# Dilated and sliding-window attention with a gated convolution layer: sequence positions reordered by residue mod 12, dilated q and k transposed without a cast, weights cast by the load, and a new order of steps

## Chip, core and metric

The kernel runs on one core of a Trainium2 chip. The metric is device time in microseconds (us) of one launch, the median of several runs. The core's engines work side by side, each through its own list of instructions: PE (TensorE: matmuls and transposes), DVE (VectorE), ACT (ScalarE), POOL (GpSimd) and SP, whose queue here only issues DMAs.

## What is computed

There are 8 batches, 8 heads, 576 positions and head size 64. Heads 0 to 3 ("plain") see the last 32 positions; heads 4 to 7 ("dilated") see every fourth of the last 128. The output of attention is x, which goes through a gate and two projections:

```python
scores = scale * np.matmul(q, k.transpose(0, 1, 3, 2))
mask_plain = (rel >= 0) & (rel < window)                                  # window 32
mask_dil = (rel >= 0) & (rel < window * dilation) & (rel % dilation == 0)  # dilation 4
attn = softmax(np.where(masks, scores, -1e9))
x = np.matmul(attn, v)              # heads side by side: (8, 576, 512)
for k in range(5):                  # causal, per channel
    gate_pre += conv_w[k] * xp[:, k:k + S, :]
out = (sigmoid(gate_pre) * (x @ w_val)) @ w_out
```

## The kernel before

The work is cut into 32 pairs of heads, four to a batch: two plain, then two dilated. Iteration i of the loop at L485 works on pair i. Each engine runs its instructions in the order in which this loop writes them, so that order is set by hand.

**Loading.** A group is the four plain or the four dilated heads of a batch. `load_group` (L99) loads a group from SP's queue, two groups ahead. q and k come as 128 partitions of four neighbouring rows (512 of 576 positions), and the last 64 positions in four small DMAs each, into `q_rest` and `k_rest`. The first two groups are loaded in halves of two heads. `prep_group` (L141) has POOL cast q and k of the next pair to bf16 and bring v into place: for plain heads a copy of 32 overlapping rows inside `vP`, for dilated heads casts into `vA` and `vB`.

**One pair.** `trans_in` (L256) transposes q and k on PE: four transposes of 128 rows (L261) and one of 64 (L266) for each; DVE copies q (L273) and ACT copies k (L278 or L280) out of PSUM. The position order after it is by residue mod 4, so a dilated head's keys are neighbours. `scores` (L291) multiplies for one half of the pair's work and ACT takes the exponential (L318); `apply_mask` (L322) multiplies with a 0/1 mask on DVE; `attn_v` (L333) multiplies with v, which carries a column of ones for the row sums; `normalize` (L350) divides on DVE (L359, L360). `trans_x` (L367) transposes x on PE (L380) and DVE copies it to `xT` (L382).

**The dense part.** For each 128-channel chunk c and half G of the positions, `conv` (L387) does the five-tap convolution as matmuls with diagonal matrices (L405) and ACT takes tanh (L413); `val` (L416) is x @ w_val (L420), multiplied with the gate on DVE (L426); `out_tile` (L432) projects 128 rows (L435), ACT copies them to `osb` (L440) and SP stores them (L446). `conv`, `val` and `out_tile` share two PSUM buffers, `ps_moe`. Once a batch's four pairs are there, its 8 `val` and 4 or 5 `out_tile` items go into a list, and `pop_dense` takes from it by a budget at three places in an iteration. In an iteration the order is: first scores, transposes of the pair before's x, its first conv, second scores, dense work, transposes of the next q, first half of attention, second conv, transposes of the next k, dense work, second half, dense work.

**At the start** POOL builds the masks, then (`setup_conv_w`, L221) the twenty diagonal matrices `conv_diag` (L232); in iteration 2 it casts the two weight matrices (L243, L245), loaded as fp32.

Of the kernel before, what the change touches and what calls it, by code (L numbers as in the profile page):

```python
# [22 lines left out]
def kernel(  # L23
# [9 lines left out]
):  # L33
    nc = tc.nc
# [5 lines left out]
    DIL = 4  # L40
    T = S // DIL
    scale = 1.0 / float(D) ** 0.5
    NCH = Dm // 128
    TM = 128
    TR = T - TM
    CP = T + 2
    NB = 6
# [3 lines left out]
    KOFF = 32  # L51
    NP = B * NCH
# [21 lines left out]
    mask_p = consts.tile([128, 4, 24], BF16, name="mask_p")  # L74
    mask_d = consts.tile([128, HB], BF16, name="mask_d")
    NKT = 3
    kTs = [consts.tile([128, KOFF + S + 16], BF16, name=f"kT{i}") for i in range(NKT)]
# [3 lines left out]
    vPs = [consts.tile([128, NB, 4, VS], FP32, name=f"vP{i}") for i in range(NVP)]  # L81
# [3 lines left out]
    vBst = [consts.tile([128, 4, 2, 64], FP32, name=f"vBst{i}") for i in range(NVD)]  # L85
    NXT = 3
    xTs = [xt_pool.tile([128, NCH, DIL, CP], BF16, name=f"xT{i}") for i in range(NXT)]
# [6 lines left out]
    w_st = [consts.tile([128, NCH, Dm], FP32, name=f"w_st{i}") for i in range(2)]  # L94
# [4 lines left out]
    def load_group(g):  # L99
        b, dil = g // 2, g % 2  # L100
        h0 = dil * 4
        t = {}
        parts = [(0, 2), (2, 4)] if g < 2 else [(0, 4)]
        for name in ("q", "k"):
            t[name] = qk_pool.tile([128, 4, 4 * D], FP32, name=f"{name}_nat")
            t[name + "r"] = qk_pool.tile([64, 4, D], FP32, name=f"{name}_rest")
        if dil:
            t["vst"] = vst_pool.tile([128, 4, 4 * D], FP32, name="v_st")
        for (a, e) in parts:
            for name, src in (("q", q), ("k", k)):  # L110
                nc.sync.dma_start(
                    out=t[name][:, a:e, :],
                    in_=src[b, h0 + a:h0 + e, 0:4 * TM, :].rearrange("h (p r) d -> p h (r d)", r=4),
                )
                for r in range(4):
                    nc.sync.dma_start(  # L116
                        out=t[name + "r"][16 * r:16 * r + 16, a:e, :],
                        in_=src[b, h0 + a:h0 + e, 4 * TM:S, :].rearrange(
                            "h (p r) d -> r p h d", r=4)[r],
                    )  # L120
            if not dil:
                vt = vPs[b % NVP]
                for h in range(a, e):
                    nc.sync.dma_start(
                        out=vt[32:128, :, h, 0:D],
                        in_=v[b, h0 + h].rearrange("(t p) d -> p t d", p=96),
                    )
            else:
                nc.sync.dma_start(
                    out=t["vst"][:, a:e, :],  # L130
                    in_=v[b, h0 + a:h0 + e, 0:4 * TM, :].rearrange("h (p r) d -> p h (r d)", r=4),
                )
                for hf in range(2):
                    nc.sync.dma_start(
                        out=vBst[b % NVD][64 * hf:64 * hf + 48, a:e, :, :].rearrange("p h j d -> p h (j d)"),
                        in_=v[b, h0 + a:h0 + e, 4 * 96:S, :].rearrange(
                            "h (p f j) d -> f p h (j d)", f=2, j=2)[hf],
                    )
        grp_tiles[g] = t

    def prep_group(g, a):  # L141

        b, dil = g // 2, g % 2
        t = grp_tiles[g]
        e = a + 2
        for name in ("k", "q"):
            if a == 0:
                t[name + "b"] = qb_pool.tile([128, 4, 4, D], BF16, name=f"{name}_b")
                t[name + "rb"] = qb_pool.tile([64, 4, D], BF16, name=f"{name}_rb")
            nc.gpsimd.tensor_copy(  # L150
                t[name + "b"][:, :, a:e, :],
                t[name][:, a:e, :].rearrange("p h (r d) -> p r h d", r=4))
            nc.gpsimd.tensor_copy(t[name + "rb"][:, a:e, :], t[name + "r"][:, a:e, :])
        if True:
            if not dil:
                vt = vPs[b % NVP]
                for h in range(a, e):
                    nc.gpsimd.tensor_copy(
                        vt[0:32, 1:NB, h, 0:D], vt[96:128, 0:NB - 1, h, 0:D])
            else:  # L160
                nc.gpsimd.tensor_copy(
                    vAs[b % NVD][:, a:e, :, 0:D],
                    t["vst"][:, a:e, :].rearrange("p h (r d) -> p h r d", r=4))
                nc.gpsimd.tensor_copy(
                    vBs[b % NVD][:, a:e, :, 0:D], vBst[b % NVD][:, a:e, :, :])

    load_group(0)
# [8 lines left out]
    for kt in kTs:  # L176
        nc.vector.memset(kt[:, 0:KOFF], 0.0)
        nc.vector.memset(kt[:, KOFF + S:], 0.0)
    for et in ets:
        nc.vector.memset(et[:, 2 * HB:], 1.0)  # L180
    nc.vector.memset(vPs[0][:, :, :, D:D + 1], 1.0 - 2.0 ** -9)
    nc.vector.memset(vPs[0][0:32, 0, :, 0:D + 1], 0.0)
# [14 lines left out]
    band(mask_p, [[1, 4], [4, 24]], 32)  # L197

    prep_group(0, 0)

    for i in range(NVD):
        nc.vector.memset(vAs[i][:, :, :, D:D + 1], 1.0)
# [353 lines left out]
```

## Time and profile before

| what | us |
|---|---|
| median of 3 runs | 262.7 |
| lowest and highest run | 261.54 and 263.8 |
| the profiled execution | 261.05 |
| its span, first to last instruction | 259.0 |
| PE busy | 204.8 (79%) |
| DVE busy | 132.8 (51%) |
| POOL busy | 109.3 (42%) |
| ACT busy | 106.5 (41%) |

The profile shows one execution. Its span is 2.05 us shorter than its time. Its 40 slices are 6.5 us each, and a digit is an engine's busy share in tenths. In rows of the time order stand start, length, engine, line, operation, and in brackets the idle time before it with what ended it; "x6" means that six such instructions are put together. In rows of waits stand the engine and line that waited, what it waited for, and total, number and longest. PEld is PE's loading of weights (the stationary operand), which runs beside matmuls. "ps_tr", "ps_sc" and "ps_moe" are PSUM buffers for transposes, for scores and attention, and for the dense part.

### The profile page before, as it was taken

The numbers are of one execution on the slowest core, as the hardware profiler recorded it, in microseconds if no ns is written. First come the engines' busy times: TensorE is split into PE (matmuls) and PEld (weight loads), VectorE is DVE, ScalarE is ACT, GpSimd is POOL, SyncE is SP. The second block draws the span as 40 slices with busy tenths as digits, with TensorE's granted clock in tenths as the row PEclk, the third lists the DMA queues.
The fourth block names the chain that finished last, engine by engine and source line by source line (L and its number), as shares of the span: only waits on it lengthen the run. The fifth ranks groups of instructions, "written<-read, shape, count | busy, mean of one in ns | idle before, by whom it ended". The sixth has DMA issues, their size and how long they took to land.

```text
span 259.0 us, 5708 instructions
## 1 busy us (share of the span) xinstructions
PE 204.8 (79%) x2117; PEld 131.8 (51%) x2132; DVE 132.8 (51%) x345; ACT 106.5 (41%) x198; POOL 109.3 (42%) x238
## 2 busy tenths in 40 slices
PE   0461586389997999899988998899889998999793
PEld 0240353255655665565556655656555655565551
DVE  5150243135657665575656565657445646665440
ACT  1221133042464345535553545264525455445312
POOL 2699908998044343625263426082626061000000
PEclk9999999999999999999999999999979999999999
DMA  3555889850758566595667564858582761112033
GB/s 93 147 163 158 231 272 288 254 136 0 213 174 225 124 188 197 147 240 172 197 185 186 166 207 128 223 152 247 170 217 48 224 191 40 48 37 67 16 81 121
DMA packets 60725, 41.28 MB, mean 159 GB/s; under 512 B 31509, under 2 KB 55061, under 8 KB 60698
## 3 DMA queue, kind: packets, MB, share of 16 engines
q1 hardware_dynamic: 60688, 40.91, 55.7%
q8 instruction: 16, 0.26, 0.4%
q14 instruction: 11, 0.09, 0.1%
q10 hardware_dynamic: 10, 0.01, 0.0%
HBM read 31.47 MB, written 9.44 MB: 158 GB/s over the span
## 4 chain that ended last, share of the span: by engine, by line
PE 68%; DVE 9%; SPq 8%; DMA 5%; ACT 3%; issue 3%; POOL 2%; POOLq 0%; ACTq 0%
PE ps_moe L405 16%; PE ps_moe L420 14%; PE ps_moe L435 12%; PE ps_tr L380 6%; DVE xT L382 5%; PE ps_sc L314 5%; PE ps_tr L261 5%; PE ps_sc L345 5%; SPq L116 5%; DMA q_rest<-in_q_dram 3%; PE ps_tr L266 3%; POOL w_out_b L245 2%; DMA q_nat<-in_q_dram 2%; PE ps_sc L310 2%; ACT kT L280 1%
## 5 line engine op out<-in xcount | busy, mean ns | idle before, releaser
L405 PE MATMUL ps_moe<-xT,conv_diag 128*128 128x288 bf16 (+1 forms) x384 | 54.2, 280 | 18.5 <-DVE xT L382 17.1
L413 ACT ACTIVATE gate<-ps_moe 128x288 bf16<-128x288 f32 x64 | 26.2, 410 | 101.7 <-PE ps_moe L405 101.7
L150 POOL CAST k_b<-k_nat 128x512 bf16<-128x512 f32 x32 | 20.7, 648 | 83.1 <-DMA k_nat<-in_k_dram 40.7
L318 ACT ACTIVATE et<-ps_sc 128x576 bf16<-128x576 f32 x64 | 41.6, 651 | 16.3 <-PE ps_sc L310 11.8
L405 PEld LDWEIGHTS <-conv_diag 128*128 128x128 bf16 x384 | 32.5, 101 | 26.7 <-issue 10.0
L426 DVE SCALAR_TENSOR_TENSOR y_all<-gate,ps_moe 128x288 bf16<-128x288 bf16 x64 | 28.4, 452 | 31.0 <-PE ps_moe L420 29.9
L420 PE MATMUL ps_moe<-xT,w_val_b 128*128 128x288 bf16 x256 | 41.7, 305 | 0.5 <-ACT osb L440 0.2
L360 DVE TENSOR_TENSOR xn<-ps_sc,rec 96x384 bf16<-96x384 f32 (+1 forms) x64 | 35.6, 555 | 2.2
L435 PE MATMUL ps_moe<-w_out_b,y_all 128*128 128x512 bf16 x129 | 35.0, 380 | 0.8
L261 PE MATMUL ps_tr<-ident,q_b 128*128 128x128 bf16 x128 | 13.8, 237 | 23.4 <-POOL q_b L150 23.4
L420 PEld LDWEIGHTS <-w_val_b 128*128 128x128 bf16 x256 | 24.1, 103 | 10.5 <-issue 2.2
L440 ACT COPY osb<-ps_moe 128x512 f32<-128x512 f32 x36 | 21.1, 585 | 18.6 <-PE ps_moe L435 16.9
L331 DVE TENSOR_TENSOR et<-et,mask_d 128x576 bf16<-128x576 bf16 x32 | 17.2, 537 | 20.1 <-ACT et L318 20.1
L382 DVE COPY xT<-ps_tr 128x576 bf16<-128x576 bf16 x32 | 14.6, 458 | 22.3 <-PE ps_tr L380 22.0
L314 PE MATMUL ps_sc<-qT,kT 64*128 64x96 bf16 (+1 forms) x320 | 20.0, 223 | 4.7 <-ACT kT L280 3.1
L273 DVE COPY qT<-ps_tr 128x576 bf16<-128x576 bf16 x32 | 14.4, 451 | 17.5 <-PE ps_tr L266 17.5
L261 PEld LDWEIGHTS <-q_b 128*128 128x128 bf16 x128 | 9.5, 105 | 26.1 <-POOL q_b L150 23.9
L331 DVE TENSOR_TENSOR et<-et,mask_p 128x576 bf16<-128x576 bf16 x32 | 16.3, 511 | 10.6 <-ACT et L318 10.1
L345 PEld LDWEIGHTS <-et 128*128 128x128 bf16 x384 | 17.7, 101 | 5.5 <-DVE et L331 0.6
L314 PEld LDWEIGHTS <-kT 64*128 64x128 bf16 x320 | 9.1, 97 | 22.1 <-issue 10.0
L380 PE MATMUL ps_tr<-ident,xn 96*128 96x96 bf16 (+2 forms) x192 | 19.8, 217 | 0.6 <-DVE xn L360 0.6
L150 POOL CAST q_b<-q_nat 128x512 bf16<-128x512 f32 x32 | 19.4, 606 | 0.0
(55 smaller groups left out, 220.8 us busy)
## 6 DMA issues: line engine op xcount, KB each, us to landing
q_nat<-in_q_dram SPq DMA_DIRECT2D x14, 512.0 KB, 4.5
k_nat<-in_k_dram SPq DMA_DIRECT2D x14, 512.0 KB, 4.8
vP<-in_v_dram SPq DMA_DIRECT2D x32, 144.0 KB, 3.4
v_st<-in_v_dram SPq DMA_DIRECT2D x7, 512.0 KB, 4.5
out_dram<-osb SPq DMA_DIRECT2D x8, 256.0 KB, 2.5
out_dram<-osb SPq DMA_DIRECT2D x8, 224.0 KB, 2.7
out_dram<-osb SPq DMA_DIRECT2D x8, 192.0 KB, 2.3
vBst<-in_v_dram SPq DMA_DIRECT2D x14, 96.0 KB, 4.1
```

What stands on the lines that cost most here:

```text
L150: nc.gpsimd.tensor_copy(t[name + "b"][:, :, a:e, :], t[name][:, a:e, :].rearrange("p h (r d) -> p r h d", r=4))
L261: nc.tensor.transpose(out=ps[:, r * T:r * T + TM], in_=t[name + "b"][:, r, a:a + 2, :], identity=ident,)
L314: nc.tensor.matmul(out=ps[:, hh, col:col + w], lhsT=lhsT, rhs=rhs, start=True, stop=True)
L318: nc.scalar.activation(out=e3, in_=ps[:, :, 0:HB], func=AF.Exp, scale=scale)
L331: nc.vector.tensor_tensor(out=e3, in0=e3, in1=m, op=ALU.mult)
L345: nc.tensor.matmul(out=ps[:, hh, j * AVS:j * AVS + D + 1], lhsT=et[:, hh * HB + col:hh * HB + col + 128], rhs=rhs, start=True, stop=True)
L360: nc.vector.tensor_tensor(out=xn[0:R, 3 * hf:3 * hf + 3, :, :].rearrange("p n h d -> p h n d"), in0=av[:, :, :, 0:D], in1=rec[0:R, :, :, N ...
L380: nc.tensor.transpose(out=o, in_=xn[0:w, 3 * hf + j, :, :], identity=ident[0:w, 0:w])
L405: nc.tensor.matmul(out=ps[:, o * T:(o + n) * T], lhsT=conv_diag[:, c, K - 1 - m, :], rhs=xt[:, c, r:r + n, off:off + T], start=(idx == 0), ...
L420: nc.tensor.matmul(out=ps[:, 0:HB], lhsT=w_val_b[:, mc, c * 128:(c + 1) * 128], rhs=xt[:, mc, 2 * G:2 * G + 2, 2:], start=(mc == 0), stop= ...
L426: nc.vector.scalar_tensor_tensor(out=y_all[:, c, b * S + G * HB:b * S + (G + 1) * HB], in0=gates.pop((b, c, G)), scalar=1.0, in1=ps[:, 0:H ...
L435: nc.tensor.matmul(out=ps, lhsT=y_all[:, c, 128 * n:128 * n + 128], rhs=w_out_b[:, c, :], start=(c == 0), stop=(c == NCH - 1),)
```

## The change

Positions are now ordered by residue mod 12, as 12 runs of 48. q and k lie in 96 partitions. For plain heads each partition holds 6 neighbouring rows of each head; POOL casts them and six transposes of 96 rows take the place of five. For dilated heads two heads lie side by side in 96 partitions of 12 rows each; there is no cast: PE transposes the upper bf16 half of every fp32 number (`hi_bf16`), two rows at a time, and the two halves of the array then hold two residues of one head, not two heads. The blocks of dilated scores are 120 and 48 wide, not 128 and 32. The small rest loads and casts are gone. For the first pair q is loaded from ACT's queue and q and k are cast on DVE. `conv_diag` is made on DVE, one product for each chunk. The weights are loaded from POOL's queue by DMAs that cast to bf16, and the factor 0.5 of w_out moves to the copy of the output. conv has 9 and 5 matmuls for its halves, where it had 6 and 6, over as many columns. An output tile is stored in runs of up to 48 rows, not 144.

The order in an iteration is now: first scores, dense work, transposes of x, second scores, a conv of the half that was queued before, k's transposes, first half of attention, the next conv, q's transposes, dense work, second half, dense work. A conv carries a time from which it may be taken.

```diff
+                (eng or nc.gpsimd).tensor_copy(
+                    t[(name, a)],
+                    t[name][:, a:e, :].rearrange("p h (j d) -> p j h d", j=6))
...
-    load_group(0)
+    load_group(0, ((0, 2),), q_eng=nc.scalar)
...
+    prep_pair(0, nc.vector)
+    load_group(0, ((2, 4),))
+    load_group(1)
...
-        for c in range(NCH):
-            for kk in range(K):
-                nc.gpsimd.tensor_scalar(
-                    out=conv_diag[:, c, kk, :], in0=ident,
-                    scalar1=conv_w_sb[:, c, kk:kk + 1], scalar2=None, op0=ALU.mult,
-                )
+    def make_conv_diag(c):
+        nc.vector.tensor_tensor(
+            out=conv_diag[:, c, :, :],
+            in0=ident[:, None, :].to_broadcast([128, K, 128]),
+            in1=conv_w_sb[:, c, :, None].to_broadcast([128, K, 128]),
+            op=ALU.mult)
...
-            nc.sync.dma_start(out=st, in_=src.rearrange("(c p) n -> p c n", p=128))
...
+            nc.gpsimd.dma_start(out=dst, in_=src.rearrange("(c p) n -> p c n", p=128))
...
+        if not dil:
+            for j in range(6):
+                nc.tensor.transpose(
+                    out=ps[:, j * 96:(j + 1) * 96], in_=t[(name, a)][:, j, :, :],
+                    identity=ident[0:96, 0:96])
+        else:
+            src = t[name].rearrange("p h x -> p (h x)")
+            pv = ps.rearrange("p (h c e u) -> p h c e u", h=2, c=2, e=3)
+            for w2 in range(6):
+                o = a * 384 + w2 * 128
+                nc.tensor.transpose(
+                    out=pv[:, :, w2 % 2, w2 // 2, :], in_=hi_bf16(src[:, o:o + 128]),
+                    identity=ident[0:96, 0:96])
...
+            r0 = 6 * G - m
+            n_wrap = max(0, -r0)
+            if n_wrap:
+                pieces.append((m, 0, W12 - n_wrap, 1, n_wrap))
+            pieces.append((m, n_wrap, max(r0, 0), 2, 6 - n_wrap))
...
-            f = 128 * n + p
-            b, r, t = f // S, (f % S) // T, f % T
-            w = min(128 - p, T - t)
+            b, w, u = f // S, (f % S) // U, f % U
+            r = min(128 - p, U - u)
...
+        dense.extend(v0 + v1[:2] + o0[:1] + v1[2:] + o0[1:] + o1)
...
+    def pop_conv(i):
+        if convs and convs[0][0] < i:
+            run(convs.pop(0)[1])
...
-        budget[0] = min(budget[0] + amount, 2.0)
-        while dense and budget[0] >= COST[dense[0][0]] * 0.5:
+        budget[0] = min(budget[0] + amount, 1.5)
+        while dense and budget[0] >= COST[dense[0][0]] * 0.6:
...
+    def push_conv(i, t):
+        b, c = pair_info(i)[0:2]
+        for G in range(2):
+            convs.append((t + 0.5 * G, ("c", b, c, G)))
...
         scores(i, 0)
-        if i > 0:
-            trans_x(i - 1)
-            pb, pc = pair_info(i - 1)[0:2]
-            convs += [("c", pb, pc, 0), ("c", pb, pc, 1)]
-            if pc == NCH - 1:
-                queue_batch(pb)
-        apply_mask(i, 0)
         if i == 0:
             setup_conv_w()
-        if i == 2:
-            cast_weights()
-        pop_conv()
+        pop_dense(0.5)
+        if i > 0:
+            trans_x(i - 1)
+            push_conv(i - 1, i)
+            if c == 0:
+                queue_batch(b - 1)
+        apply_mask(i, 0)
+        if i < NCH:
+            make_conv_diag(i)
         scores(i, 1)
-        pop_dense(0.5)
+        pop_conv(i)
         apply_mask(i, 1)
         if i + 1 < NP:
-            trans_in(i + 1, "q")
+            trans_in(i + 1, "k")
         attn_v(i, 0)
         normalize(i, 0)
-        pop_conv()
+        pop_conv(i + 0.5)
         if i + 1 < NP:
-            trans_in(i + 1, "k")
+            trans_in(i + 1, "q")
         pop_dense(0.5)
         attn_v(i, 1)
         normalize(i, 1)
-        pop_dense(0.97)
+        pop_dense(1.0)
```

Three places show how instructions move. A number behind a name tells buffers apart. First POOL at the start, from the end of pair 1's preparation on (the `vP` copy) to that of pair 2 (`k_nat_194` and `v_st_196` are its loads). Before:

```order
L158 COPY vP0_107<-vP0_107 32x5x64 x2
L232 TENSOR_SCALAR conv_diag_121<-ident_96,conv_w_sb_120 128x128 x20
L150 CAST k_b_358<-k_nat_194 128x4x128
L153 CAST k_rb_359<-k_rest_195 64x128
L150 CAST q_b_362<-q_nat_192 128x4x128
L153 CAST q_rb_363<-q_rest_193 64x128
L161 CAST vA0_109<-v_st_196 128x8x64
```

Now, from pair 1's casts of k and q to pair 2's v:

```order
L147 CAST k_b_199<-k_nat_123 96x768
L147 CAST q_b_201<-q_nat_122 96x768
L151 COPY vP0_107<-vP0_107 32x2x5x64
L184 MEMSET mask_d_99 128x120
L185 AFFINE_SELECT mask_d_99<-mask_d_99 128x120
L189 AFFINE_SELECT mask_d_99<-mask_d_99 128x120
L214 COPY mask_d_99<-mask_d_99 128x120
L184 MEMSET mask_d_99 128x48
L237 DMA w_val_b_120<-in_moe_w_val_dram 128x4x512
L237 DMA w_out_b_121<-in_moe_w_out_dram 128x4x512
L154 CAST vA0_109<-v_st_162 128x8x64
```

The twenty `conv_diag` products and pair 2's casts of q and k have left POOL; the mask for dilated heads and the two weight loads now stand between pair 1's and pair 2's preparation.

Second SP's queue, the loads of group 1 (dilated heads of batch 0). Before, the first of its two halves:

```order
L111 DMA q_nat_192<-in_q_dram 128x2x256
L116 DMA q_rest_193<-in_q_dram 16x2x64 x4
L111 DMA k_nat_194<-in_k_dram 128x2x256
L116 DMA k_rest_195<-in_k_dram 16x2x64 x4
L129 DMA v_st_196<-in_v_dram 128x2x256
L134 DMA vBst0_113<-in_v_dram 48x2x128 x2
```

Now all of it, with the first load of group 2 behind:

```order
L126 DMA k_nat_161<-in_k_dram 96x2x768
L126 DMA q_nat_160<-in_q_dram 96x2x768
L130 DMA v_st_162<-in_v_dram 128x4x256
L134 DMA vB_st_163<-in_v_dram 64x4x128 x2
L113 DMA k_nat_194<-in_k_dram 96x4x384
```

Twenty-six issues have become five, and k goes first.

Third PE in iteration 5 (the second plain pair of batch 1), at the transposes of x (`xn`); of each kind of instruction the first is shown, the repeats are left out. Before:

```order
L435 MATMUL ps_moe_786<-w_out_b_123,y_all_118 128x512
L314 LDWEIGHTS kT2_102
L314 MATMUL ps_sc_805<-qT_741,kT2_102 128x96
L380 LDWEIGHTS xn_749
L380 MATMUL ps_tr_813<-ident_96,xn_749 128x4x24
L405 LDWEIGHTS conv_diag_121
L405 MATMUL ps_moe_822<-xT1_116,conv_diag_121 128x288
L314 LDWEIGHTS kT2_102
L314 MATMUL ps_sc_831<-qT_741,kT2_102 128x96
```

Now:

```order
L287 MATMUL ps_sc_666<-qT_623,kT2_102 128x96
L412 LDWEIGHTS w_val_b_120
L412 MATMUL ps_moe_674<-xT0_113,w_val_b_120 128x288
L379 LDWEIGHTS xn_600
L379 MATMUL ps_tr_680<-ident_96,xn_600 128x12x8
L287 LDWEIGHTS kT2_102
L287 MATMUL ps_sc_689<-qT_623,kT2_102 128x96
L397 LDWEIGHTS conv_diag_119
L397 MATMUL ps_moe_697<-xT0_113,conv_diag_119 128x288
L256 LDWEIGHTS k_nat_352
```

Before, the conv behind the transposes reads what they wrote (`xT1`, batch 1). Now a val group stands ahead of the transposes and the second scores behind them, and the conv that follows reads `xT0`: it is the last conv of batch 0. The last row is the next, dilated, pair's k, loaded as weights straight from the fp32 load.

More of the change, by code (lines that the diff above doesn't have):

```diff
@@ L121, in load_group @@
[L121 to L128, printed above, removed]
+                    out=t["k"][:, a:e, :],
+                    in_=k[b, a:e].rearrange("h (p j) d -> p h (j d)", j=6))
+                for f in range(2):
+                    q_eng.dma_start(
+                        out=t["q"][48 * f:48 * f + 48, a:e, :],
+                        in_=q[b, a:e].rearrange("h (u f j) d -> f u h (j d)", f=2, j=6)[f])
@@ L139, in load_group, with prep_pair @@
[L139 to L143 removed]
+                        out=t["vBst"][64 * f:64 * f + 64, a:e, :, :].rearrange("p h j d -> p h (j d)"),
+                        in_=v[b, 4 + a:4 + e, 4 * TB:S, :].rearrange(
+                            "h (p f j) d -> f p h (j d)", f=2, j=2)[f])
+    def prep_pair(i, eng=None):
+        b, c, dil, g, a = pair_info(i)
         t = grp_tiles[g]
         e = a + 2
[L146 to L165, printed above, removed]
@@ L439, in out_tile @@
         osb = out_pool.tile([128, Dm], FP32, name="osb")
-        nc.scalar.copy(out=osb, in_=ps)
+        nc.scalar.mul(out=osb, in_=ps, mul=0.5)
         p = 0
```

315 lines of the change are left out of this document (152 added, 163 removed).

## The prediction

> **What bounds the kernel now.** I read first the page's head and slices, then busy time by stage, then the waits, then the order of time at the start and in one regular iteration. The page shows an engine mix that changes:
>
> ```profile
> span 259.0 us, 5708 instructions
> PE   0461586389997999899988998899889998999793
> POOL 2699908998044343625263426082626061000000
> ```
>
> For its first quarter the span shows a busy POOL and a half-empty PE; afterwards PE is at 9 and POOL is slack. Cutting the span where iterations begin (an iteration begins with its first scores, six L314 matmuls, or four in a dilated pair) gives the stages:
>
> ```profile
> 20.00:28.70 8.70, 0.45 (x7) 0.21 (x6) 0.46 (x1) 1.01 (x2) 8.70 (x17) 1.00 0.65 182
> 43.60:49.40 5.80, 0.02 (x4) 0.00 (x0) 0.46 (x1) 0.65 (x1) 5.80 (x8) 1.00 0.69 195
> 64.50:237.20 172.70, 154.61 (x1716) 101.42 (x1728) 104.04 (x261) 84.67 (x159) 60.43 (x132) 0.99 0.58 163
> 237.20:259.00 21.80, 14.96 (x116) 8.47 (x116) 6.77 (x17) 6.32 (x12) 0.00 (x0) 1.00 0.28 84
> ```
>
> Columns: length, then busy us (and instructions) of PE, its weight loads, DVE, ACT and POOL, then clock, DMA share, GB/s. Two stretches have PE empty and POOL full. In the regular stage, 26 iterations, PE is busy 154.61 of 172.70 us, DVE 104.04, ACT 84.67: PE is the bound, with 18 us idle. The waits name both:
>
> ```profile
> PE ps_tr L261 <- POOL q_b L150: 23.4, 4, 8.3
> PE ps_moe L405 <- DVE xT L382: 17.1, 31, 0.6
> ```
>
> The start in order of time (start, length, engine, line):
>
> ```profile
> 8.13 0.61 PE L261 MATMUL ps_tr<-ident,q_b 128*128 128x128 bf16 x4 [8.13 <-POOL q_b L150]
> 10.34 0.42 PE L314 MATMUL ps_sc<-qT,kT 64*128 64x96 bf16 x6 [0.73 <-ACT kT L280]
> 15.43 11.92 POOL L232 TENSOR_SCALAR conv_diag<-ident,conv_w_sb 128x128 bf16<-128x128 bf16 x20
> 16.31 0.42 PE L314 MATMUL ps_sc<-qT,kT 64*128 64x96 bf16 x6 [0.29 <-ACT kT L280]
> 27.30 0.61 POOL L150 CAST k_b<-k_nat 128x512 bf16<-128x512 f32 x1
> 28.75 0.61 PE L261 MATMUL ps_tr<-ident,q_b 128*128 128x128 bf16 x4 [8.30 <-POOL q_b L150]
> 32.48 0.40 PE L314 MATMUL ps_sc<-qT,kT 64*128 64x128 bf16 x4 [0.29 <-ACT kT L278]
> 39.72 0.40 PE L314 MATMUL ps_sc<-qT,kT 64*128 64x128 bf16 x4 [0.29 <-ACT kT L278]
> 42.16 5.85 POOL L245 TENSOR_SCALAR w_out_b<-w_st 128x512 bf16<-128x512 f32 x4 [0.43 <-DMA w_st<-in_moe_w_out_dram]
> 49.41 0.61 PE L261 MATMUL ps_tr<-ident,q_b 128*128 128x128 bf16 x4 [5.79 <-POOL q_b L150]
> 53.15 0.42 PE L314 MATMUL ps_sc<-qT,kT 64*128 64x96 bf16 x6 [0.29 <-ACT kT L280]
> 55.04 1.36 PE L405 MATMUL ps_moe<-xT,conv_diag 128*128 128x288 bf16 x6 [0.55 <-DVE xT L382]
> ```
>
> Casts that PE needs stand behind twenty conv_diag products (11.92) and behind the weight casts (5.85). The iterations start at 10.34, 16.31, 32.48, 39.72, 53.15 and, below, 64.52. Now a regular iteration:
>
> ```profile
> 64.52 0.30 PE L314 MATMUL ps_sc<-qT,kT 64*128 64x96 bf16 x6
> 64.76 0.43 PE L380 MATMUL ps_tr<-ident,xn 96*128 96x96 bf16 x6
> 65.74 0.80 PE L405 MATMUL ps_moe<-xT,conv_diag 128*128 128x288 bf16 x6 [0.55 <-DVE xT L382]
> 66.47 0.30 PE L314 MATMUL ps_sc<-qT,kT 64*128 64x96 bf16 x6
> 67.20 0.39 PE L261 MATMUL ps_tr<-ident,q_b 128*128 128x128 bf16 x4
> 67.52 0.20 PE L266 MATMUL ps_tr<-ident,q_rb 64*128 64x64 bf16 x1
> 67.65 0.37 PE L345 MATMUL ps_sc<-vP,et 128*128 128x65 bf16 x6
> ```
>
> The same six conv matmuls last 1.36 at 55.04 and 0.80 at 65.74, though the clock column says 1.00 at both: by its own durations PE ran near half speed until about 61 us. So lost time at the start is lost at the slow rate too.
>
> **The change, term by term.** Base: this execution's 261.05 us, a span of 259.0 plus 2.05 around it. The median of the runs, 262.7, is 1.65 above it.
>
> *The start (iterations 0 to 4, now until 64.52).* What fed it, and the size of one large load:
>
> ```profile
> 0.80 0.45 SPq L111 DMA_DIRECT2D q_nat<-in_q_dram  x1
> 1.30 1.85 SPq L116 DMA_DIRECT2D q_rest<-in_q_dram  x4
> 5.98 0.61 POOL L150 CAST k_b<-k_nat 128x512 bf16<-128x512 f32 x1 [3.79 <-DMA k_nat<-in_k_dram]
> 28.70:43.60 14.90, 13.17 (x112) 8.24 (x112) 5.82 (x15) 4.87 (x9) 7.35 (x14) 1.00 0.91 285
> w_st<-in_moe_w_out_dram SPq DMA_DIRECT2D x1, 1024.0 KB, 8.7
> ```
>
> SP needed five issues of some 0.46 us for q before k went out at 3.19, and k was there at 5.98, 2.8 later. The change issues k first, q on ACT's queue, one DMA instead of five, and pair 0 is cast by DVE. K should land near 4 us instead of 6. The DVE cast of 768 elements is not in the trace: below, the 0.46 of L382's 576-element copy (quoted in the rivals); above, POOL's 0.61 x 768/512 = 0.92. I take 0.8, as fp32 in is nearest to POOL's cast. Two of them, six transposes and copies: first scores at 6.5 instead of 10.34.
>
> Iteration 0 lasted 5.97 (16.31 - 10.34). Pair 1's POOL casts, 0.92 each, now come before the mask work, and there is no rest cast: 4.3. Iteration 1 lasted 16.17; 8.30 was the conv_diag queue, which leaves POOL for DVE as four products, and one conv group (1.36 slow) moves to a later iteration: 6.4. A conv_diag product of 640 elements on DVE lies between 0.46 and 1.0 by the same copy; it stands between the two mask multiplies and is covered by PE's transposes and conv. Iteration 2 has no such wait, 7.24; slow shorter transposes (twice 0.2) go, a wait for the normalized x with no other work to cover it comes: 7.1. Iteration 3 lasted 13.43 with 5.79 of waiting for the weight casts, which the DMA now does: 7.2. Iteration 4 lasted 11.37; less the xT wait: 11.0. Sum 6.5 + 4.3 + 6.4 + 7.1 + 7.2 + 11.0 = 42.5 against 64.52, **-22**.
>
> Does data hold it up? PE's transposes of pair 2 now wait for the load itself, with attention and scores queued behind them. Up to q of pair 2, 20 heads of 147 KB, 2.95 MB, must land; at the 285 GB/s of the busiest stage 10.4 us and some 3 for the first, so 13.5, about when PE asks (pair 2's k at 12, q at 15). Group 2 is behind 3.7 MB and shares with 2.1 MB of weights: all by 29, its k first, needed at 27. The weights, issued from POOL's queue ahead of pair 2's v casts, have until 36; a load of 1 MB took 8.7. No cast by DMA is in the trace; at twice 8.7 it is still in time. So 0 here, +6 at the far end. Far below: 38, if the clock rises one iteration early.
>
> *A regular iteration.* It lasts 172.72/26 = 6.643 (64.52 to 237.24). The six transposes of xn follow one another every (0.43 - 0.216)/5 = 0.043, so they need 0.26, yet conv starts 0.98 after them: copy latency and copy. Then conv to scores is 0.73, of which about 0.62 is work and 0.11 the turn to 64-row matmuls. In the new order the second scores follow the transposes and the old conv follows those: 0.26 + 0.11 and later 0.62 instead of 0.98 + 0.73. **-0.72.** Loads of q and k as 96-partition blocks: q's transposes took 67.65 - 67.20 = 0.45, of which the 64-row one costs most by its turns; six of 96 need 0.26, and k the same. **-0.38.** Conv gets 14 matmuls for 12 with the same 2880 columns: 0.01. Dilated pairs lose their POOL casts, all hidden already. That makes 5.54. What comes back: five of a batch's eight val groups now stand in one iteration, each needs a DVE product before one of two PSUM buffers is free, and all stand behind normalize; I estimate 0.9 per four iterations, and 0.1 per iteration for transposes of x that find no dense work ahead. **5.8**; DVE's 104.04/26 = 4.0 and ACT's 3.26 fit in. Ends: 5.45, if other small waits go too, and 6.2, if over half comes back. 26 x 5.8 = 150.8 instead of 172.7, **-22**.
>
> *The end* lasts 21.8; the shorter last iteration takes 1.3, two more output issues of 0.46 give 0.9: 21.4. Elsewhere the stores, 120 pieces for 56, cost SP 120 x 0.46 = 55 us of some 200; the loads queued behind them go out two groups, over 20 us, ahead of use and land in under 9, so I count 0.
>
> Sum: 42.5 + 150.8 + 21.4 + 2.05 = 216.8. I forecast **217**. Ends: 38 + 141.7 + 20.5 + 2 = 202; 48.5 + 161.2 + 22 + 2 = 234.
>
> **Rivals.**
>
> ```profile
> 65.22 0.46 DVE L382 COPY xT<-ps_tr 128x576 bf16<-128x576 bf16 x1 [0.68 <-PE ps_tr L380]
> L261 PEld LDWEIGHTS <-q_b 128*128 128x128 bf16 x128 | 9.5, 105 | 26.1 <-POOL q_b L150 23.9
> L345 PE MATMUL ps_sc<-vP,et 128*128 128x65 bf16 x192 | 12.2, 202 | 0.0
> L345 PE MATMUL ps_sc<-vA,et 128*128 128x65 bf16 x128 | 9.8, 201 | 0.3 <-DVE et L331 0.3
> ```
>
> *A new wait for DVE takes the place of the old.* The mask multiply is behind the xT copy, and attention needs it 1.3 us later. The time is scores, conv and six transposes, 0.3 + 0.62 + 0.26 and a turn. For: DVE's rows come in program order and DVE will be 70% busy. Against: 0.46 + 0.5 and a hand-over fit in 1.3. If it ate 0.5 each: 217 + 13 = 230. Chance 0.15.
>
> *Fine-grained operands slow PE.* Dilated q/k are transposed from every second bf16 of fp32 (192 weight loads on 16 pairs), x is written to PSUM in runs of 8, scores read runs of 8. For: no strided weight load is in the trace. Against: V read at every second element costs 202, packed V 201, and runs of 24 (L380) need 0.043 per 96 columns. Bounds: 0, and a load of 105 ns no longer hidden, 12 x (0.105 - 0.043) x 16 = 12 us; with twice the x transposes (0.26 x 32 = 8) 237. Likely half: 227. Chance 0.10. [...]
>
> *The start is bound by transfer,* at the 182 GB/s of the stretch from 20.00: pair 4's k and q, behind 4.9 MB and half of the weights, land at 36 instead of by 30; +6, 223. Chance 0.12.
>
> *PE warms early.* If the denser start lifts the rate by iteration 2, two iterations fall from 7.2 to about 4.5 and iteration 4 to 7.5: 208. Chance 0.12. [...]
>
> *Slower than before: PE stays at the slow rate.* Iteration 4, slow, took 11.37 where a regular one takes 6.64 and would take 5.8. Each extra slow iteration costs some 5.6; from nine on the kernel is slower than 261, with twelve it is 217 + 67 = 284. The place is iterations 4 to 15, if small gaps keep PE below what lifts it. Against: today's iterations with a 0.55 gap keep the fast rate. Chance 0.02.
>
> *Nothing gained,* because DMA paces all: 0.58 of the regular stage speaks against. 261. Chance 0.01.
>
> **Numbers.** The forecast holds 0.48; the others as given. 202 to 234 leaves out the slow, the unchanged and both far ends. A measurement of this kernel tells about 1% from no change; faster by more: 0.97, within 1%: 0.01, slower: 0.02.
>
> **What would show it.** First scores near 6.5; no wait of PE for POOL over 1 us; iteration 4 begins near 31.5, iteration 5 near 42.5; then 5.8 per iteration; the wait of conv for xT gone but in the last pair; transposes of q and k 0.26 us apart. It is wrong if iterations stay over 6.2, if strided weight loads space the dilated transposes over 0.06, or if PE waits for loads.

## The result, and the profile after

| | us |
|---|---|
| changed kernel, median of 4 runs (lowest, highest) | 207.53 (206.76, 208.66) |
| before, 4 runs on the same chip | 263.25 (261.54, 264.46) |
| ratio, 95% interval | 0.789, 0.783 to 0.795 |
| profiled execution; its span | 207.24; 205.5 |
| forecast (range) | 217.0 (202 to 234) |

The kernel is 56 us faster, 9.5 us more than forecast. First the page's head and slices; a slice is now 5.1 us:

```profile
span 205.5 us, 5689 instructions
PE   0579884999899999999899999998999999999960
POOL 3473305147041243013430352116131344000000
DMA  6999999999959997499979998699959996523043
```

The half-empty quarter of PE is gone, and POOL is slack from the beginning. The DMA row is new: it reads 9 nearly everywhere. By stage (length, then PE, its weight loads, DVE, ACT, POOL, then clock, DMA share, GB/s):

```profile
8.50:39.50 31.00, 24.82 (x289) 18.99 (x290) 20.43 (x47) 12.40 (x23) 12.22 (x22) 0.94 1.14 241
39.50:181.00 141.50, 137.86 (x1829) 99.76 (x1828) 105.63 (x262) 83.78 (x158) 42.27 (x64) 1.00 0.92 209
181.00:205.50 24.50, 16.92 (x134) 9.87 (x133) 7.03 (x17) 8.02 (x15) 0.00 (x0) 0.90 0.31 87
```

In the 26 regular iterations PE is busy 137.86 of 141.50 us; before it was 154.61 of 172.70. The DMA share there rose from 0.58 to 0.92, though about as many bytes move. The first stage moves 241 GB/s, less than the 285 that the prediction counted on. The start in order of time:

```profile
5.10 0.56 DVE L147 CAST k_b<-k_nat 96x768 bf16<-96x768 f32 x1 [2.79 <-DMA k_nat<-in_k_dram]
6.72 0.56 DVE L147 CAST q_b<-q_nat 96x768 bf16<-96x768 f32 x1 [1.07 <-DMA q_nat<-in_q_dram]
8.55 0.42 PE L287 MATMUL ps_sc<-qT,kT 64*128 64x96 bf16 x6 [0.55 <-DVE qT L261]
13.40 0.43 PE L287 MATMUL ps_sc<-qT,kT 64*128 64x96 bf16 x6 [0.54 <-DVE qT L261]
18.18 0.38 PE L295 MATMUL ps_sc<-qT,kT 64*128 64x120 bf16 x4 [0.22 <-DVE qT L261]
24.05 0.28 PE L295 MATMUL ps_sc<-qT,kT 64*128 64x120 bf16 x4 [0.36 <-DVE qT L261]
28.57 0.30 PE L287 MATMUL ps_sc<-qT,kT 64*128 64x96 bf16 x6 [0.57 <-DVE qT L261]
32.01 0.71 POOL L151 COPY vP<-vP 32x640 f32<-32x640 f32 x1 [6.29 <-DMA vP<-in_v_dram]
33.66 0.66 PE L248 MATMUL ps_tr<-ident,k_b 96*128 96x96 bf16 x6 [2.80 <-POOL k_b L147]
34.46 1.39 PE L397 MATMUL ps_moe<-xT,conv_diag 128*128 128x288 bf16 x9
39.46 0.30 PE L287 MATMUL ps_sc<-qT,kT 64*128 64x96 bf16 x6
```

Iterations 0 to 5 begin at 8.55, 13.40, 18.18, 24.05, 28.57 and 39.46. One long wait of PE is left, 2.80 at 33.66: k of pair 5 is cast behind the copy of `vP`, and that copy waited 6.29 for v of batch 1. After it PE runs at half rate again: the clock column reads 0.51 from 33.40 to 36.90, and nine conv matmuls take 1.39 (0.80 at 80.14, where it reads 1.00). A regular iteration:

```profile
78.03 0.30 PE L287 MATMUL ps_sc<-qT,kT 64*128 64x96 bf16 x6
78.27 0.74 PE L379 MATMUL ps_tr<-ident,xn 120*128 120x120 bf16 x6
78.82 0.32 PE L287 MATMUL ps_sc<-qT,kT 64*128 64x96 bf16 x6
79.07 0.79 PE L397 MATMUL ps_moe<-xT,conv_diag 128*128 128x288 bf16 x5
83.30 0.30 PE L287 MATMUL ps_sc<-qT,kT 64*128 64x96 bf16 x6
```

The second scores follow the transposes, the conv behind them waits for nothing; before, conv began 0.98 after the transposes. What PE waits for in these 26 iterations (total, number, longest):

```profile
PE ps_tr L379 <- DVE xn L359: 1.9, 3, 0.7
PE ps_moe L412 <- DVE y_all L418: 1.2, 7, 0.2
```

And the end, where SP's stores run on behind the last output copy (198.76 + 0.60):

```profile
198.76 0.60 ACT L432 ACTIVATE osb<-ps_moe 128x512 f32<-128x512 f32 x1 [0.27 <-PE ps_moe L427]
```
```profile
181.77 20.95 SPq L438 DMA_DIRECT2D out_dram<-osb  x27
```

Against the terms of the prediction:

| stage | before | forecast | after |
|---|---|---|---|
| iteration 5 begins | 64.52 | 42.5 | 39.46 |
| 26 regular iterations (each) | 172.7 (6.643) | 150.8 (5.8) | 141.6 (5.445) |
| the end | 21.8 | 21.4 | 24.5 |

The regular stage, worked out from the starts of all its matmuls (each counted until the next begins, summed by line, then compared): the transposes of x and the wait behind them take 17.6 us less, the transposes of q and k 9.1 less, all others together 4.4 less.

### The profile page after: what moved, and what is told of

It reads as the page before. It is cut to its first block, busy times and chain, and to the rows that moved or that the text cites. A ratio compares the mean times of both kernels' runs of the same rounds, so it can differ in the third digit from the quotient of the medians.

```text
span 205.5 us, 5689 instructions
## 1 busy us (share of the span) xinstructions
PE 180.9 (88%) x2260; PEld 129.6 (63%) x2260; DVE 136.4 (66%) x344; ACT 106.1 (52%) x198; POOL 57.2 (28%) x98
## 4 chain that ended last, share of the span: by engine, by line
PE 68%; DMA 15%; DVE 10%; issue 2%; ACT 1%; POOL 0%; SPq 0%; ACTq 0%; POOLq 0%; DVEq 0%
PE ps_moe L397 18%; PE ps_moe L427 15%; PE ps_moe L412 12%; DMA vP<-in_v_dram 9%; PE ps_tr L379 6%; PE ps_sc L340 5%; DVE y_all L418 5%; DMA k_nat<-in_k_dram 4%; PE ps_tr L256 3%; PE ps_tr L248 3%; PE ps_sc L295 2%; DVE xn L359 2%; DMA q_nat<-in_q_dram 2%; PE ps_sc L306 2%; PE ps_sc L287 1%
## 5 line engine op out<-in xcount | busy, mean ns | idle before, releaser
L397 PE MATMUL ps_moe<-xT,conv_diag 128*128 128x288 bf16 (+4 forms) x448 | 53.0, 260 | 0.2 <-ACT osb L432 0.2
L412 PE MATMUL ps_moe<-xT,w_val_b 128*128 128x288 bf16 x256 | 39.9, 287 | 1.6 <-DVE y_all L418 1.2
L427 PE MATMUL ps_moe<-w_out_b,y_all 128*128 128x512 bf16 x144 | 36.5, 379 | 0.0
L432 ACT ACTIVATE osb<-ps_moe 128x512 f32<-128x512 f32 x36 | 21.5, 597 | 28.0 <-PE ps_moe L427 25.4
L147 POOL CAST k_b<-k_nat 96x768 bf16<-96x768 f32 x15 | 12.6, 843 | 38.1 <-DMA k_nat<-in_k_dram 37.7
L154 POOL CAST vA<-v_st 128x512 bf16<-128x512 f32 x16 | 10.2, 635 | 38.9 <-DMA v_st<-in_v_dram 38.9
L354 DVE RECIPROCAL rec<-ps_sc 96x6 f32<-96x6 f32 (+1 forms) x64 | 12.1, 190 | 10.7 <-PE ps_sc L340 10.0
L379 PEld LDWEIGHTS <-xn 96*128 96x128 bf16 (+2 forms) x192 | 12.9, 98 | 9.6 <-DVE xn L359 3.9
L151 POOL COPY vP<-vP 32x640 f32<-32x640 f32 x16 | 11.7, 732 | 23.4 <-DMA vP<-in_v_dram 19.3
L427 PEld LDWEIGHTS <-y_all 128*128 128x128 bf16 x144 | 12.0, 97 | 9.7 <-issue 0.3
```

What stands on the lines that cost most here:

```text
L379: nc.tensor.transpose(out=o, in_=xn[0:w, z, n, :, :], identity=ident[0:w, 0:w])
L397: nc.tensor.matmul(out=ps[:, o * U:(o + n) * U], lhsT=conv_diag[:, c, K - 1 - m, :], rhs=xt[:, c, r:r + n, off:off + U], start=(idx == 0), ...
L412: nc.tensor.matmul(out=ps[:, 0:HB], lhsT=w_val_b[:, mc, c * 128:(c + 1) * 128], rhs=xt[:, mc, 6 * G:6 * G + 6, 2:], start=(mc == 0), stop= ...
L427: nc.tensor.matmul(out=ps, lhsT=y_all[:, c, 128 * n:128 * n + 128], rhs=w_out_b[:, c, :], start=(c == 0), stop=(c == NCH - 1),)
L432: nc.scalar.mul(out=osb, in_=ps, mul=0.5)
```

## Experiments

Four questions: is it the order that shortens the regular iteration; is it POOL's work that emptied PE at the start; what paces the start now; and what makes the end longer.

**The old order in the changed kernel.**

```diff
-        pop_dense(0.5)
         if i > 0:
             trans_x(i - 1)
-            push_conv(i - 1, i)
+            push_conv(i - 1, 0)
...
+        pop_conv(i + 1)
         scores(i, 1)
-        pop_conv(i)
+        pop_dense(0.5)
```

> The changed kernel with only the order of the steps put back: transposes of x, at once the conv that reads them, second scores, dense work; no due times for conv; everything else stays. Theory (the order carries most of the 5.445 us iteration, because conv no longer waits for DVE's copy of x): the wait of conv for xT comes back at 0.5 to 0.6 each, plus the turns around it, 0.5 to 0.72 per iteration; 26 iterations 13 to 19 longer, kernel 219 to 227 us. Rival (the shorter transposes and loads carry it, and the order only moves slack): under 0.15 per iteration, 207 to 212 us.

Measured: 226.61 us (225.71 to 228.71); 26 iterations take 162.8 us in its profile (39.86 to 202.70), 21.3 more than in the changed kernel. The wait is back:

```profile
PE ps_moe L397 <- DVE xT L380: 14.3, 26, 0.6
```

Counted from start to start, the transposes of x and the wait behind them take 17.6 us of the 21.3, as much as they lost in the change; 14.3 of that is this row. Two stretches at half rate (60.05 to 63.46 and 111.25 to 114.66) cost some 1.7 each, half of their 3.41. The first, in iteration 8 (the granted clock stands behind the five engines):

```profile
57.07:60.05 2.98, 2.04 (x28) 1.42 (x28) 1.43 (x4) 0.81 (x2) 1.31 (x3) 1.00 0.45 131
60.05:63.46 3.41, 3.41 (x22) 2.34 (x21) 1.25 (x3) 0.79 (x2) 0.00 (x0) 0.50 0.78 187
```

Small waits come close together, PE is busy 2.04 of 2.98 us, and the clock is halved for the next 3.41. Two iterations that do the same work, 16 and 24, show what that costs:

```profile
107.66:117.09 9.43, 8.23 (x83) 5.91 (x81) 5.58 (x15) 3.06 (x6) 2.71 (x5) 0.82 0.78 181
158.50:166.52 8.02, 6.76 (x83) 4.94 (x81) 5.32 (x15) 3.05 (x6) 1.80 (x4) 1.00 0.70 178
```

Both have two waits of PE close together, 0.65 for xn and 0.55 for xT. In iteration 16 the clock fell behind them, in iteration 24 it did not, and the difference is 1.4 us. What decides that is not shown. The theory holds; the order is worth about 19 us of the 56 (226.61 against 207.53).

**The start's two POOL edits alone, in the kernel before.**

```diff
-                nc.gpsimd.tensor_scalar(
-                    out=conv_diag[:, c, kk, :], in0=ident,
+        nc.vector.tensor_tensor(
+            out=conv_diag[:, c, :, :],
...
-            nc.sync.dma_start(out=st, in_=src.rearrange("(c p) n -> p c n", p=128))
+            nc.gpsimd.dma_start(out=dst, in_=src.rearrange("(c p) n -> p c n", p=128))
```

> The kernel before with two parts of the change alone: conv_diag as four products on DVE, and the weights loaded by POOL's queue with a cast (0.5 of w_out in the output copy). Order, tiling and loads stay. Theory (the casts queued behind these on POOL were what emptied PE at the start): the 8.3 and 5.8 us waits of PE for POOL go, iteration 5 begins at 46 to 50 instead of 64.5, regular iterations stay at 6.6, kernel 243 to 249 us. Rival (the loads or PE's slow rate held the start as much): iteration 5 not before 53, kernel 251 to 257.

Measured: 250.92 us (249.77 to 253.82), ratio 0.964 (0.953 to 0.974); iteration 5 begins at 55.03. The theory said 46 to 50; the rival, not before 53, holds (its time, 251 to 257, by its lower edge), and too much was put down to POOL's own work. POOL is free now, and its casts wait for loads:

```profile
17.91 0.61 POOL L149 CAST k_b<-k_nat 128x512 bf16<-128x512 f32 x1 [0.76 <-DMA k_nat<-in_k_dram]
23.30 0.29 POOL L152 CAST k_rb<-k_rest 64x128 bf16<-64x128 f32 x1 [4.77 <-DMA k_rest<-in_k_dram]
```
```profile
24.20 0.61 PE L261 MATMUL ps_tr<-ident,q_b 128*128 128x128 bf16 x4 [4.12 <-POOL q_b L149]
```

In pair 2 the small rest loads, issued last and four to a tensor, come 5 us behind the large one, and PE waits 4.12 for the cast of q that stands behind them. In pairs 0 and 1 they came only 0.32 and 0.27 behind. At pair 2 the weights' loads, issued on POOL's queue at 15.53 and 16.41, are under way beside them; no run separates the two causes. So of the 25 us of the start, 9.5 come from POOL's two edits alone; the other 15.5 need the rest of the change (new tiles without rest loads, first pair, order) on top.

**Packed copies of dilated q and k.**

```diff
+            for name in ("k", "q"):
+                t[(name, a)] = qb_pool.tile([96, 12 * D], BF16, name=f"{name}_d")
+                nc.gpsimd.tensor_copy(
+                    t[(name, a)],
+                    t[name].rearrange("p h x -> p (h x)")[:, a * 384:a * 384 + 768])
...
-                    out=pv[:, :, w2 % 2, w2 // 2, :], in_=hi_bf16(src[:, o:o + 128]),
+                    out=pv[:, :, w2 % 2, w2 // 2, :], in_=src[:, o:o + 128],
```

> The changed kernel, but POOL casts dilated q and k to packed bf16 tiles first, and PE transposes those, in place of every second bf16 of the fp32 load. Theory (a weight load from every second element costs PE nothing): transposes of dilated q and k start 0.043 us apart as before, the 26 regular iterations stay within 1 us of 141.6; the start changes by -1 to +3, because 32 casts of 0.84 join POOL's queue; kernel 206 to 211. Rival (strided weight loads cost PE): regular iterations get shorter, by 4 to 12 us in all, kernel 196 to 204.

Measured: 209.93 us (208.97 to 212.09). The regular iterations take 143.6, 2.0 more than without the copies, where the theory said within 1. Weight loads of the changed kernel (every second element) and of this one (packed), mean ns last before the second bar:

```profile
L256 PEld LDWEIGHTS <-k_nat 96*128 96x128 bf16 x72 | 4.4, 97 | 0.6
```
```profile
L261 PEld LDWEIGHTS <-k_d 96*128 96x128 bf16 x66 | 4.0, 97 | 0.6
```

Both take 97 ns. Strided loading of weights costs nothing here; the copies that it saves make the regular stage 2 us longer, and no wait in that stage accounts for it.

**PE kept busy from the beginning.**

```diff
+    filler(36)
     trans_in(0, "k")
+    filler(8)
     trans_in(0, "q")
+    filler(8)
```

> The changed kernel with matmuls of the identity, whose results nobody reads, added on PE: 36 before the first transposes, 8 behind each of the first two, and 8 twice in iterations 0 and 1, so that PE is busy from about 1.5 us. Theory (the start is paced by what has landed, and v of the second batch lands at 32 whatever PE does): PE's rate doubles some 10 us sooner, iterations 1 and 2 get shorter, the wait for the cast of pair 5's k grows by as much, iteration 5 begins between 38.5 and 40.5 and the kernel takes 206 to 209. Rival (PE's slow rate paces the start): iteration 5 begins 3 to 5 us earlier, kernel 202 to 204.5.

Measured: 207.11 us (206.81 to 209.19). The granted clock is recorded as full from 5.9 (in the changed kernel from 23.2), and six transposes of q take 0.43 at 7.55 (0.66 at 7.34 in the changed kernel). Iteration 4 begins at 28.09 instead of 28.57, but:

```profile
33.60 0.66 PE L248 MATMUL ps_tr<-ident,k_b 96*128 96x96 bf16 x6 [2.76 <-POOL k_b L147]
...
39.30 0.30 PE L287 MATMUL ps_sc<-qT,kT 64*128 64x96 bf16 x6
```

Iteration 5 begins at 39.30, as before (39.46). PE's rate does not pace the start. The wait for the cast of pair 5's k, which was to grow by what PE gained, stayed at 2.76; of the 1.4 us by which iteration 3 began sooner (22.62), 0.99 went into a wait for the cast of q at 27.11.

**The casts ahead of the copies that wait for v.**

```diff
-            for name in ("k", "q"):
-                t[(name, a)] = qb_pool.tile([96, 6, 2, D], BF16, name=f"{name}_b")
+            heads = [a] if b == 0 else ([0, 2] if a == 0 else [])
+            for h0 in heads:
+                for name in ("k", "q"):
```

> The changed kernel with one order on POOL changed from the second batch on: the casts of k and q of both plain pairs of a batch stand ahead of the two vP copies, which wait for v. Theory (PE's 2.8 us wait at 30.9, and the half-rate stretch behind it, come from a cast queued behind a copy that waits for v): k of pair 5 is transposed at about 31, attention then waits for the vP copy until about 32.8; iteration 5 begins 1 to 3 us earlier than 39.46, kernel 204.5 to 206.5. Rival (PE's end of the start is set by v itself, and the wait only moves from the transposes to attention): iteration 5 within 0.8 us of 39.46, kernel 206.5 to 208.5.

Measured: 208.11 us (205.81 to 211.64); iteration 5 at 38.86. The rival holds. The `vP` copies start at 32.50, PE's transposes of k no longer wait, but attention needs `vP`:

```profile
32.80 0.69 PE L250 MATMUL ps_tr<-ident,k_b 96*128 96x96 bf16 x6
33.29 0.60 PE L342 MATMUL ps_sc<-vP,et 128*128 128x65 bf16 x6
```

**The weights two iterations later.**

```diff
-            load_weights()
+        if i == 2:
+            load_weights()
```

> The changed kernel with the two weight loads issued from POOL's queue two iterations later (near 19.5 instead of 13.9). Theory (the first 40 us are paced by what has landed): v of the second batch lands 2.5 to 4 us earlier, PE's wait for the cast of pair 5's k shrinks from 2.8 to under 1, PE keeps its full rate, iteration 5 begins at 34 to 36.5, kernel 202.5 to 205. Rival (the transfers do not share one rate, so v comes when it did): iteration 5 within 1 us of 39.46; or the weights now come too late for the first val and add up to 3 us, kernel up to 211.

Measured: 207.50 us (204.13 to 212.16). In its profile:

```profile
28.21 0.72 POOL L151 COPY vP<-vP 32x640 f32<-32x640 f32 x1 [2.83 <-DMA vP<-in_v_dram]
```
```profile
30.65 0.42 PE L248 MATMUL ps_tr<-ident,k_b 96*128 96x96 bf16 x6
...
35.03 0.30 PE L287 MATMUL ps_sc<-qT,kT 64*128 64x96 bf16 x6
```

v is there 3.8 us sooner, PE keeps its full rate (nine conv matmuls take 0.80 at 31.15), and iteration 5 begins 4.4 us earlier, as the theory said. So the landing of v paces the end of the start, and the weights' loads were in its way; whether by their bytes or because the DMA casts them is not separated. But the median does not move, and the theory's 202.5 to 205 for the kernel fails: the regular iterations take 145.7 instead of 141.6. Part of that shows as waits:

```profile
137.04 0.43 PE L248 MATMUL ps_tr<-ident,k_b 96*128 96x96 bf16 x6 [0.71 <-POOL k_b L147]
...
139.61 0.43 PE L248 MATMUL ps_tr<-ident,q_b 96*128 96x96 bf16 x6 [1.31 <-POOL q_b L147]
```

These loads were issued at 130, though the program puts them at the start of iteration 20 (117.5). On SP's queue 13 output stores stand ahead of them, of some 0.46 each, and 4.3 us of waits for earlier loads to land. I had called 120 stores for 56 free; they cost the loads much of their lead.

**Stores of the last four tiles over three queues.**

```diff
+            if n == 35:
+                eng = nc.scalar
+            elif n >= 32 and piece % 2:
+                eng = nc.gpsimd
+            else:
+                eng = nc.sync
```

> The changed kernel with the stores of the last four output tiles spread: every second piece of tiles 32 to 34 from POOL's queue, tile 35 from ACT's, the rest from SP's. Theory (the end is 3 us longer than forecast because SP issues three or four pieces of 0.46 per tile and runs 3.4 us behind the last output copy): the last store is issued by about 201 instead of 202.7 and the span ends 1.3 to 2.3 us earlier, kernel 205 to 206.3. Rival (the stores' landing, not their issue, sets the end): within 0.6 us of the changed kernel.

Measured: 206.12 us (204.80 to 207.88). From the last iteration's first scores (181.74) to the end of the span it takes 22.6 instead of 24.5, and the last store is issued at 201.4 instead of 202.7:

```profile
200.07 1.30 ACTq L445 DMA_DIRECT2D out_dram<-osb  x3
```

The theory holds: two of the three us by which the end was under-forecast are SP's issues. This rests on the profile; the time alone is not clear of the changed kernel's.

**Loads by themselves.** For the DMA share of 0.92.

```diff
+    plan = [(128, 4, 256, rows128), (96, 4, 384, rows96), (96, 2, 768, flat(96, 2, 768)),
+            (128, 4, 384, flat(128, 4, 384)), (96, 4, 256, flat(96, 4, 256)), (128, 2, 768, flat(128, 2, 768))]
```

> A kernel that only loads: six stages, one after the other, of six loads each, by partitions and bytes of one packet: 128 x 1 KB (the shape before), 96 x 1.5 KB and 96 x 3 KB (the shapes now), 128 x 1.5 KB, 96 x 1 KB, 128 x 3 KB; then it stores zeros; all computation is left out. Theory (loads into 96 of the 128 partitions are slower, which is why a packet of the changed kernel takes longer and its DMA share rose from 0.56 to 0.84): at the same packet size 96 partitions move at about three quarters of the rate of 128: some 240 GB/s against 300 or more. Rival (only the packet's size and the other queues matter): 96 and 128 within 5% at the same size.

Six windows, one inside each stage in the order of the list; the last number is GB/s:

```profile
3.00:12.00 9.00, 0.00 (x0) 0.00 (x0) 1.00 0.98 322
15.00:29.00 14.00, 0.00 (x0) 0.00 (x0) 1.00 1.04 233
32.00:45.00 13.00, 0.00 (x0) 0.00 (x0) 1.00 0.97 245
48.00:60.00 12.00, 0.00 (x0) 0.00 (x0) 1.00 1.06 378
63.00:73.50 10.50, 0.00 (x0) 0.00 (x0) 1.00 1.04 209
77.00:88.00 11.00, 0.00 (x0) 0.00 (x0) 1.00 0.99 393
```

At equal packets 96 partitions move 209, 233 and 245 GB/s where 128 move 322, 378 and 393: 0.62 to 0.65. Larger packets give part of it back: 128 partitions of 1 KB, the old shape, ran at 322, and 96 partitions of 1.5 and 3 KB, the new tiles, at 233 and 245, which is about three quarters. The theory had three quarters at equal packets; the direction is right, the difference is larger. The 241 GB/s of the changed kernel's start are what such loads reach alone.

**The changed kernel again, loads three groups ahead, and three edits together.** These ran beside one another.

```diff
     load_group(1)
+    load_group(2)
...
-        if c % 2 == 0 and g + 2 < 2 * B:
-            load_group(g + 2)
+        if c % 2 == 0 and g + 3 < 2 * B:
+            load_group(g + 3)
```

> The changed kernel once more, on the chip of the next two, so that they can be set against it: 207 to 208.5 us.

> The changed kernel with every group of loads issued three groups ahead of use instead of two. Theory (in the regular stage transfers are hidden anyway; only the spread between runs comes from loads that stand behind stores on SP's queue and now and then land late): start and regular iterations within 1 us of the changed kernel, time 206 to 208.5, no run above 210. Rival (loads that come late cost PE time in every run): 202 to 205.

> Three edits together: weights two iterations later, stores of the last four tiles over three queues, loads three groups ahead. If the start is paced by what has landed and the end by SP's issues, their gains add up: 4.4 from the start and 1.9 from the end, 200 to 202.5 us. If the third edit puts more load traffic ahead of v of the second batch, the first gain is lost in part: 203 to 206.

Measured: 207.77 (206.91 to 210.08), 210.61 (208.47 to 212.13) and 208.93 us (207.33 to 209.37). Loads further ahead made the kernel 1.4% longer, which neither theory had, and which is hardly more than the scatter; in its profile the regular iterations take 144.3 where the changed kernel's second profile has 141.2. The third kernel missed both its ranges. In it the two known gains are there (iteration 5 at 35.90, the end 22.7), but iteration 12 takes 12.24 us. In that iteration, on SP, ACT and PE:

```profile
70.14 2.75 SPq L446 DMA_DIRECT2D out_dram<-osb  x4
```
```profile
78.99 0.60 ACT L433 ACTIVATE osb<-ps_moe 128x512 f32<-128x512 f32 x1 [4.77 <-DMA out_dram<-osb]
```
```profile
80.67 0.51 PE L341 MATMUL ps_sc<-vP,et 128*128 128x65 bf16 x6 [4.02 <-DVE et L325]
```

These four stores were issued behind four loads of together 1.9 MB (67.20 to 69.98), which landed from 72.56 to 77.89. The stores took 6.2 to 7.9 us to land, where a median store of 96 KB takes 2.1 in the changed kernel. So the four output buffers came free late; ACT stood 4.77 us before an output copy, until the store issued at 72.58 had landed at 78.75, and the exponential behind that copy was what PE needed. The wait on one queue went through three engines. The loads behind the stores were late too: SP's DMAs take turns over eight semaphores, as the traces' instructions show (100 and 102 to 108 in the kernel before and in the changed one), and the load of q at 77.50 waited until v_st, issued at 68.17, had landed (POOL's cast that waited for v_st began at 77.16).

**Weights later and stores spread, loads as they were.**

> The changed kernel with two edits: weights two iterations later, stores of the last four tiles over three queues; loads two groups ahead as they were. If the gains add up, iteration 5 begins near 35, the part from the last iteration on takes 22.6, and the kernel takes 201 to 203 us. If the earlier start only brings PE sooner to loads that stand behind stores on SP's queue, PE waits for casts of q or k in one or two regular iterations and 1.5 to 3 us are given back: 203.5 to 206.

Measured: 203.13 us over 7 runs (202.08 to 208.50), ratio to before 0.777 (0.773 to 0.781), where the changed kernel has 0.789 (0.783 to 0.795) and 0.796 (0.790 to 0.802). It beats both kernels. Its profiled execution is one of the longer, 207.56: iteration 5 begins at 35.49 and the end takes 22.6, as expected, but the 26 regular iterations take 147.7 instead of 141.6. Of these 6.1 us, casts that came late are 2.2:

```profile
PE ps_tr L248 <- POOL q_b L147: 1.2, 2, 0.7
...
PE ps_tr L248 <- POOL k_b L147: 1.0, 1, 1.0
```

Another 1.5 is a wait in iteration 28, with a lower clock behind it (the page's clock row reads 8 from 164.6 to 174.9); that iteration takes 8.53 instead of 5.28. The expectation's second case, a gain given back through late casts, is so seen in part. The median lies between its two ranges. How much the runs near 202 give back is open: they have no profile here.

## Why the prediction was right, and where its sizes were off

*Regular iteration, 5.8 against 5.445.* The mechanism was right: -0.72 for the order was 17.6/26 = 0.68, and undoing the order brought the wait back in all 26 iterations. -0.38 for the transposes of q and k was 9.1/26 = 0.35. The term that failed is "what comes back: 0.9 per four iterations, and 0.1 per iteration". That is 0.325, though only 0.26 was added (5.54 to 5.8). Those waits measured 0.12 (val 1.2 us in 26 iterations, the transposes of x 1.9), and with them counted in, all other matmuls still got 0.17 shorter, 4.4 us together. Of these, some 1.7 are a half-rate stretch (190.85 to 194.26) of the kernel before,

```profile
188.00:198.00 10.00, 9.30 (x75) 5.84 (x76) 5.47 (x14) 3.24 (x6) 4.88 (x12) 0.83 0.55 135
```

which the changed kernel has nowhere in this stage. The other 2.7 are not assigned.

*The start, 42.5 against 39.46.* The sum came within 3 us by errors that cancel. First scores came 2 us late (8.55, not 6.5). "K should land near 4 us" was one step that failed: k took 4.3 from its issue at 0.81, not 2.8, and the cast of q then waited 1.07 more for q. Why k took longer is not tested; its load now has 96 partitions, and others run beside it. DVE's cast was 0.56, not 0.8. Iteration 0 took 4.85 for 4.3. Iterations 1 to 3 took 4.78, 5.87 and 4.52 instead of 6.4, 7.1 and 7.2, since too much of the old waiting was left in them and the clock rose at 23.2 (six transposes of dilated q or k take 0.69 at 20.95 and 0.53 at 22.97; six of a plain pair take 0.42 at 26.30). Iteration 4 was right by luck, 10.89 for 11.0: not slow work from end to end, but a wait of 2.80 for v and 3.4 us at half rate behind it. So the paragraph "Does data hold it up?" failed too. It counted 285 GB/s, group 2 "all by 29" and 0 us of waiting; the stage moved 241, v of batch 1 landed at 31.9, and PE waited for it, which is one of the prediction's own signs of being wrong.

*The end, 21.4 against 24.5.* "Two more output issues of 0.46": SP was already behind. Three or four pieces of 0.46 per tile are 1.4 to 1.8 us, and PE makes a tile in 0.87.

*The rivals.* "PE warms early" happened in part: the clock rose at 23.2 and iteration 3 took 4.52, but iteration 4 stayed at 10.89, and the filler run shows that a still earlier rise gives nothing (full from 5.9, iteration 5 at 39.30). The measured 207.5 lies at this rival's 208 by another way, the shorter regular iterations. "Bound by transfer" happened in another place, v of batch 1 instead of q and k of pair 4, because the weights' loads were under way beside it. "Fine-grained operands" is refuted: strided weight loads take 97 ns like packed ones, and the transposes that write PSUM in runs of 8 last 0.42 for six, against 0.43 before in runs of 24:

```profile
40.42 0.42 PE L379 MATMUL ps_tr<-ident,xn 96*128 96x96 bf16 x6
```

The wait on DVE was at most 0.7. Of "what would show it", first scores and "no wait of PE for POOL over 1 us" failed, and the sign "if PE waits for loads" came once; the rest came as written or better.

## What to carry to other kernels

Put the wait between a copy and its reader under work that is ready (worth 17.6 us here), and look at the clock row when small waits stand close together: they can cost more than their length (1.4 us more here, once of two like cases). SP's queue, which issues both loads and stores, made each wait for the other (loads of iteration 20 went out at 130 instead of 117.5; an output copy stood 4.77 us), so count every issue on it and the DMAs that may be under way at once, and look for what a gain at the start will run into later. When PE waits at the start, ask which bytes have landed, and what else was under way (v came 3.8 us sooner without the weights' loads beside it), before making an engine faster.

## What the runs showed of the hardware

- Loads into 96 partitions ran at 0.62 to 0.65 of the rate into 128, for packets of 1, 1.5 and 3 KB: 209, 233 and 245 GB/s against 322, 378 and 393. What makes the difference is not shown.
- With the old order, the granted clock fell to half at 60.05, after 2.98 us in which PE was still busy for 2.04; waits of PE of 0.36, 0.40 and 0.55 us had ended at 57.07, 57.77 and 59.06. Waits of 0.65 and 0.55 went ahead of a fall in iteration 16 and of none in iteration 24, so no threshold is shown. The stretches of half rate in iterations 8 and 16 lasted 3.41 us each.
- A DVE cast of 96 x 768 from fp32 to bf16 took 0.56 us, POOL's 0.82.
